# The first layer's activation: ScalarE reads the product bank twice, VectorE adds from SBUF, GpSimd's step is gone

## The chip, the cores and the metric

The kernel runs on one core of a Trainium2 chip. Its time is the device time of one execution, in microseconds (us). The time before is the median of three runs; the profile is of one more execution.

## What is computed

Three stages follow one another. The first is a delta-rule attention over 4 batches, 8 heads, 768 steps and 48 features per head, worked in twelve chunks of 64 steps. Its output, 3072 tokens of 384 features, goes through two feed-forward layers with 2048 hidden features each. The change touches the activation of the first of them:

```python
def _moe_ref(x, w_in, w_out):
    h = x @ w_in                                    # 3072x384 by 384x2048
    g = np.where(h > 0.0, h, 1.0 * (np.exp(np.minimum(h, 0.0)) - 1.0))
    return g @ w_out                                # 2048x384

def _moe2_ref(x, w_in, w_out, a, b):
    h = x @ w_in
    P = a[0] + a[1]*h + a[2]*h*h + a[3]*h*h*h
    Q = 1.0 + abs(b[0])*abs(h) + abs(b[1])*h*h
    return (P / (Q + 1e-6)) @ w_out
```

## The kernel before

The tokens are cut into six windows of 512 (two chunks each). While the first layer works on window w, the attention of window w+1 (`chain`, lines 401 to 556) and the preparation of window w+2 (`g_list` and the recurrence `t_pieces`, lines 267 to 374) run in between. The second layer comes after the sixth window.

In a window the 2048 hidden features are 16 blocks of 128, counted by f. For each block five functions are called:

- `H` (line 581) multiplies: nine matmuls of 512 columns (lines 577 to 579), because operands are split into a high and a low part, into a bank of `h_a`. Its two banks (and in the sixth window a third, `h_c`) are used in turn; both banks of `h_a` are one tile.
- `A1` (line 601): ScalarE reads the bank and writes e = relu(-h) (line 605), then e = exp(-e) (line 606); GpSimd, called POOL, subtracts one in place (line 607).
- `B1` (line 609): VectorE reads the bank again and writes e = max(h, 0) + e (line 612). This is the last read of the bank.
- `C1` (line 614): ScalarE rounds e to gh (line 618), VectorE writes the remainder gl = e - gh (line 620). In the second window POOL writes it for half of the blocks.
- `O` (line 588) multiplies gh and gl with the block of the second weight: nine matmuls (lines 595 to 597) that accumulate in three banks `o`. It stands about two blocks behind `H`.

`e`, `gh` and `gl` have two buffers each. `wo_split` (line 563) splits a block of the second weight for `O` (ScalarE, line 70, and POOL, line 71). Weights arrive as 64-bit numbers; `conv_x`, `conv_d` and `conv_s` (lines 154 to 195) turn them into 32-bit ones with ScalarE, VectorE and, for the first layer, POOL. The second layer's weights are turned in the windows: w_out in windows two to five, w_in all in the sixth.

Each call has a due time in the table `Q` and the loops of lines 811 to 871; the calls are sorted by it. Up to the first steps of the second layer a scheduler then puts the instructions of each engine in order, by due order and its own estimate of when an engine is free, so a change of one instruction can move others. Each engine runs its list strictly in order.

Of the kernel before, what the change touches and what calls it, by code (L numbers as in the profile page):

```python
# [7 lines left out]
F32 = mybir.dt.float32  # L8
# [3 lines left out]
AF = mybir.ActivationFunctionType  # L12
ALU = mybir.AluOpType
# [23 lines left out]
def kernel(  # L37
# [16 lines left out]
    nc = tc.nc  # L54
    mm = nc.tensor.matmul
    act = nc.scalar.activation
# [4 lines left out]
    mp = ctx.enter_context(tc.tile_pool(name="mp", bufs=2))  # L61
# [506 lines left out]
    hp = {}  # L568
# [30 lines left out]
    et = {}  # L599

    def A1(key, f, NC):
        ps = hp[key, f][:, 0:NC]
        e = mp.tile([128, 512], F32, tag="e", name="e")[:, 0:NC]
        et[key, f] = e
        act(out=e, in_=ps, func=AF.Relu, scale=-1.0)  # L605
        act(out=e, in_=e, func=AF.Exp, scale=-1.0)  # L606
        nc.gpsimd.tensor_scalar(out=e, in0=e, scalar1=1.0, scalar2=-1.0, op0=ALU.mult, op1=ALU.add)  # L607

    def B1(key, f, NC):
        ps = hp.pop((key, f))[:, 0:NC]  # L610
        e = et[key, f]
        nc.vector.scalar_tensor_tensor(out=e, in0=ps, scalar=0.0, in1=e, op0=ALU.max, op1=ALU.add)  # L612

    def C1(key, f, NC):
        e = et.pop((key, f))
        gh = mp.tile([128, 512], F32R, tag="gh", name="gh")
        gl = mp.tile([128, 512], F32R, tag="gl", name="gl")
        act(out=gh[:, 0:NC], in_=e, func=AF.Copy)  # L618
        eng = nc.gpsimd if (f % 4 < Q["pg0"] if key == 0 else key == 1 and f % 4 < Q["pg1"]) else nc.vector
        eng.tensor_tensor(out=gl[:, 0:NC], in0=e, in1=gh[:, 0:NC].bitcast(F32), op=ALU.subtract)  # L620
        gt[key, f] = gh, gl
# [189 lines left out]
    for w in range(NW):  # L811
        T = 16 * w
        NC = 256 * len(WINS[w])
        at(T + Q["sx"], split_x, w)
        for f in range(NF):
            at(T + f, lambda w=w, f=f, NC=NC: H(w, f, xt[w], NC))
            at(T + f + .05, A1, w, f, NC)
            at(T + f + Q["b1"], B1, w, f, NC)
            at(T + f + Q["c1o"], C1, w, f, NC)
            at(T + f + Q["ws"], wo_split, w, f)  # L820

            def o1(w=w, f=f, NC=NC):
                t = oring.pop((w, f))
                O(w, f, t[:, 0], t[:, 1], NC)
            at(T + (f + 2.4 if f < NF - 2 else f + 1.95 if f == NF - 2 else f + 1.4), o1)
# [145 lines left out]
```

## Time and profile before

| | us |
|---|---|
| median of three runs | 1167.28 (1157.68 to 1171.71) |
| the profiled execution | 1167.12 |
| its span, first to last instruction | 1165.3 |
| first layer, six windows | about 114 to 758 of the span |
| second layer | about 758 to 1165 |
| TensorE, VectorE, ScalarE, POOL busy | 1061.5, 899.7, 740.7, 520.4 |

PE is TensorE's matmuls, PEld its weight loads, DVE VectorE, ACT ScalarE. A row of waits names the engine and line that stood idle, the one that released it, the total, how often, and the longest. In a row of the timeline the idle time before it stands in brackets. Matmuls overlap: each is shown with 0.39 us while the next one starts 0.23 us after it, so a short stall of TensorE shows in the weight loads rather than in the matmuls.

### The profile page before, as it was taken

Reading aid. Unit: us, or ns where it says so; the run is one execution under the profiler, and the core shown is the slowest. Engines: PE = TensorE matmul, PEld = TensorE weight load, DVE = VectorE, ACT = ScalarE, POOL = GpSimd, SP = SyncE. Lnnn points to the kernel's source line nnn. Section 1 sums busy time; section 2 is a strip of 40 time slices with the busy share of each in tenths; the row PEclk is TensorE's granted clock in tenths of the full one; section 3 lists DMA queues with packets and bytes.
Section 4 is the critical chain, followed back from the end, with each engine's and each line's share of the span. In section 5 each row is a group of like instructions: output and inputs, shape, how many; then the busy total and the mean of one; then the engine's idle time right before and its main releaser. Section 6 shows DMA issues by size and latency. Waiting matters only on the chain.

```text
span 1165.3 us, 20668 instructions
## 1 busy us (share of the span) xinstructions
PE 1061.5 (91%) x7952; PEld 843.8 (72%) x7952; DVE 899.7 (77%) x1231; ACT 740.7 (64%) x1425; POOL 520.4 (45%) x496
## 2 busy tenths in 40 slices
PE   7179887898898999998999998999999999999997
PEld 7055676676687778786777766778787888878785
DVE  4987859768955883696343369999999999999996
ACT  5566666666476546554564578976766667666664
POOL 1484737433444343342443356646363454536332
PEclk8567879998899999998999999999999999999999
DMA  9534424363454122320212044400101001010000
GB/s 278 156 122 152 137 77 131 100 193 100 119 167 149 48 73 89 99 72 8 78 40 67 1 129 136 123 28 1 55 1 30 26 1 55 1 55 1 28 1 27
DMA packets 51842, 91.75 MB, mean 79 GB/s; under 512 B 7072, under 2 KB 29728, under 8 KB 51744
## 3 DMA queue, kind: packets, MB, share of 16 engines
q1 hardware_dynamic: 51744, 90.43, 25.2%
q8 instruction: 62, 1.02, 0.4%
q14 instruction: 36, 0.29, 0.1%
HBM read 77.83 MB, written 12.58 MB: 78 GB/s over the span
## 4 chain that ended last, share of the span: by engine, by line
PE 52%; DVE 23%; issue 7%; ACT 6%; DMA 6%; POOL 5%; POOLq 0%; SPq 0%; DVEq 0%; ACTq 0%
PE o L719 11%; PE h_a L577 6%; PE h_a L578 6%; PE h_a L579 6%; DVE tmp L344 4%; PE o L595 3%; PE o L596 3%; PE o L597 3%; DVE wo L691 2%; PE gp L278 2%; DVE tt L345 2%; PE cb L459 2%; PE h_b L579 2%; PE h_b L577 2%; PE h_b L578 2%
## 5 line engine op out<-in xcount | busy, mean ns | idle before, releaser
L705 POOL TENSOR_TENSOR gl<-wo 128x1024 fp32r<-128x1024 f32 x48 | 146.1, 3043 | 218.4 <-DVE wo L704 187.2
L577 PE MATMUL h_a<-xh,wi 128*128 128x512 f32 x417 | 177.8, 426 | 36.9 <-DVE e L612 33.4
L578 PE MATMUL h_a<-xl,wi 128*128 128x512 f32 x417 | 169.9, 407 | 1.4 <-DVE xl L396 1.4
L579 PE MATMUL h_a<-xh,wi 128*128 128x512 f32 x417 | 169.3, 406 | 0.0
L607 POOL TENSOR_SCALAR e<-e 128x512 f32<-128x512 f32 x96 | 65.8, 685 | 213.2 <-ACT e L606 208.3
L719 PE MATMUL o<-gh,wo 128*128 128x512 f32 x576 | 142.3, 395 | 6.7 <-ACT ys L724 6.4
L71 POOL TENSOR_TENSOR wor<-wo,wor 128x384 fp32r<-128x384 f32 x96 | 103.9, 1083 | 81.2 <-ACT wor L70 74.7
L719 PEld LDWEIGHTS o<-gh,wo 128*128 128x128 f32 x576 | 107.8, 189 | 33.7 <-ACT ys L724 11.1
L612 DVE SCALAR_TENSOR_TENSOR e<-h_a,e 128x512 f32<-128x512 f32 x91 | 62.5, 687 | 89.7 <-POOL e L607 89.0
L577 PEld LDWEIGHTS h_a<-xh,wi 128*128 128x128 f32 x417 | 81.8, 196 | 64.9 <-DVE e L612 41.7
L595 PE MATMUL o<-gh,wor 128*128 128x512 f32 x288 | 119.2, 414 | 0.2 <-ACT gh L618 0.2
L596 PE MATMUL o<-gl,wor 128*128 128x512 f32 x288 | 115.4, 401 | 3.0 <-DVE gl L620 3.0
L597 PE MATMUL o<-gh,wor 128*128 128x512 f32 x288 | 114.2, 397 | 0.0
L605 ACT ACTIVATE e<-h_a 128x512 f32<-128x512 f32 x91 | 54.1, 595 | 89.8 <-PE h_a L579 89.1
L620 DVE TENSOR_TENSOR gl<-e,gh 128x512 fp32r<-128x512 f32 x88 | 74.7, 849 | 29.2 <-ACT gh L618 28.7
L578 PEld LDWEIGHTS h_a<-xl,wi 128*128 128x128 f32 x417 | 82.0, 197 | 17.6 <-DVE xl L396 3.0
L579 PEld LDWEIGHTS h_a<-xh,wi 128*128 128x128 f32 x417 | 81.7, 196 | 18.0
L692 ACT ACTIVATE wo<-wo 128x1024 f32<-128x1024 f32 x48 | 51.0, 1064 | 65.4 <-DVE wo L691 65.4
L691 DVE SCALAR_TENSOR_TENSOR wo<-wo 128x1024 f32<-128x1024 f32 x48 | 75.9, 1582 | 8.5 <-ACT wo L684 8.5
L618 ACT ACTIVATE gh<-e 128x512 fp32r<-128x512 f32 x96 | 60.2, 627 | 32.4 <-DVE e L612 30.7
L70 ACT ACTIVATE wor<-wo 128x384 fp32r<-128x384 f32 x96 | 49.7, 519 | 47.3 <-PE o L597 42.3
L719 PE MATMUL o<-gl,wo 128*128 128x512 f32 x288 | 74.9, 396 | 2.7 <-POOL gl L705 2.7
(162 smaller groups left out, 2474.9 us busy)
## 6 DMA issues: line engine op xcount, KB each, us to landing
kv<-c_kv SPq DMA_DIRECT2D x24, 576.0 KB, 4.3
gin<-g_in SPq DMA_DIRECT2D x69, 192.0 KB, 2.8
kq<-c_kq SPq DMA_DIRECT2D x22, 512.0 KB, 3.8
raw<-w_out SPq DMA_DIRECT2D x42, 192.0 KB, 2.6
raw<-w_in SPq DMA_DIRECT2D x34, 192.0 KB, 2.4
wo<-w_in SPq DMA_DIRECT2D x30, 192.0 KB, 3.0
xr<-x2d SPq DMA_DIRECT2D x6, 768.0 KB, 5.8
out_t<-ys SPq DMA_DIRECT2D x18, 256.0 KB, 2.2
```

The lines of the kernel that those rows point to most:

```text
L71: eng.tensor_tensor(out=t[:, 1], in0=src, in1=t[:, 0].bitcast(F32), op=ALU.subtract)
L577: mm(out=ps, lhsT=hi, rhs=xh[:, c, 0:NC], start=(c == 0), stop=False)
L578: mm(out=ps, lhsT=hi, rhs=xl[:, c, 0:NC], start=False, stop=False)
L579: mm(out=ps, lhsT=lo, rhs=xh[:, c, 0:NC], start=False, stop=(c == 2))
L595: mm(out=ps[:, 0:NC], lhsT=hi[:, cs], rhs=gh[:, 0:NC], start=(f == 0), stop=False)
L596: mm(out=ps[:, 0:NC], lhsT=hi[:, cs], rhs=gl[:, 0:NC], start=False, stop=False)
L597: mm(out=ps[:, 0:NC], lhsT=lo[:, cs], rhs=gh[:, 0:NC], start=False, stop=(f == NF - 1))
L607: nc.gpsimd.tensor_scalar(out=e, in0=e, scalar1=1.0, scalar2=-1.0, op0=ALU.mult, op1=ALU.add)
L620: eng.tensor_tensor(out=gl[:, 0:NC], in0=e, in1=gh[:, 0:NC].bitcast(F32), op=ALU.subtract)
L691: v.scalar_tensor_tensor(out=sq, in0=sq, scalar=1.0 + 1e-6, in1=ab, op0=ALU.add, op1=ALU.add)
L705: nc.gpsimd.tensor_tensor(out=gl, in0=sq, in1=ab, op=ALU.mult)
L719: mm(out=ps, lhsT=wo2[2 * j + i][:, int(p == 1), cs], rhs=(gl if p == 2 else gh)[:, n], start=(j == 0 and p == 0 and i == 0), stop=(j == N ...
```

## The change

`A1` has ScalarE read the bank a second time, for p = relu(h) into a new tile `pe` with two buffers, ahead of the exponential. POOL's subtraction is gone. `B1` reads e and p, both in SBUF, and writes (e - 1) + p; it no longer reads the bank. In the changed kernel the two reads are lines 606 and 607 and the exponential is line 608; lines 612, 618 and 620 keep their numbers.

```diff
     def A1(key, f, NC):
-        ps = hp[key, f][:, 0:NC]
+        ps = hp.pop((key, f))[:, 0:NC]
         e = mp.tile([128, 512], F32, tag="e", name="e")[:, 0:NC]
-        et[key, f] = e
+        p = mp.tile([128, 512], F32, tag="pe", name="pe")[:, 0:NC]
+        et[key, f] = e, p
         act(out=e, in_=ps, func=AF.Relu, scale=-1.0)
+        act(out=p, in_=ps, func=AF.Relu)
         act(out=e, in_=e, func=AF.Exp, scale=-1.0)
-        nc.gpsimd.tensor_scalar(out=e, in0=e, scalar1=1.0, scalar2=-1.0, op0=ALU.mult, op1=ALU.add)
 
     def B1(key, f, NC):
-        ps = hp.pop((key, f))[:, 0:NC]
-        e = et[key, f]
-        nc.vector.scalar_tensor_tensor(out=e, in0=ps, scalar=0.0, in1=e, op0=ALU.max, op1=ALU.add)
+        e, p = et[key, f]
+        nc.vector.scalar_tensor_tensor(out=e, in0=e, scalar=-1.0, in1=p, op0=ALU.add, op1=ALU.add)
 
     def C1(key, f, NC):
-        e = et.pop((key, f))
+        e, _ = et.pop((key, f))
```

The lists of the engines change in two ways that matter here. On TensorE, in the second window before block 12, the block's first matmul (`wi_1880` is the block's weight, `gp` a product of the preparation, `o` the accumulators) waits before for VectorE:

```order
L596 MATMUL o_2893<-gl,wor 128x512
L597 MATMUL o_2893<-gh,wor 128x512
L278 MATMUL gp<-gin 128x128 [waits DMAHW0_49,PE_49]
L278 MATMUL gp<-gin 128x128
L278 MATMUL gp<-gin 128x128 [waits DMAHW1_49]
L278 MATMUL gp<-gin 128x128
L577 MATMUL h_a<-xh,wi_1880 128x512 [waits DVE_49]
```

and now, with the block's weight under the name `wi_1888`, for ScalarE:

```order
L596 MATMUL o_2912<-gl,wor 128x512
L597 MATMUL o_2912<-gh,wor 128x512
L278 MATMUL gp<-gin 128x128 [waits DMAHW0_49,PE_49]
L278 MATMUL gp<-gin 128x128
L278 MATMUL gp<-gin 128x128 [waits DMAHW1_49]
L278 MATMUL gp<-gin 128x128
L577 MATMUL h_a<-xh,wi_1888 128x512 [waits Activation_49]
```

The neighbours are the same; from the second to the fifth window `H`, `O` and the pieces of `chain` keep nearly the same order on TensorE, while in the first and the sixth some trade places. The wait in front of `H` has passed from VectorE to ScalarE.

On ScalarE, in the sixth window, one block before reads (`raw` are weights being turned, `wor` and `wo` splits of second weights, `wi` splits of the second layer's first weight):

```order
L605 ACTIVATE e<-h_a 128x512
L161 ACTIVATE raw_7574<-raw_7574 128x192
L606 ACTIVATE e<-e 128x512
L70 ACTIVATE wor<-wo_94 128x384
L70 ACTIVATE wi_7680<-ce 128x192
L159 ACTIVATE raw<-raw 128x192
L161 ACTIVATE raw<-raw 128x192
L70 ACTIVATE wi_7680<-ce 128x192
L618 ACTIVATE gh<-e 128x512
L605 ACTIVATE e<-h_c 128x512
```

and now a block reads:

```order
L606 ACTIVATE e<-h_a 128x512
L607 ACTIVATE pe<-h_a 128x512
L608 ACTIVATE e<-e 128x512
L159 ACTIVATE raw<-raw 128x192
L161 ACTIVATE raw<-raw 128x192
L70 ACTIVATE wi_7710<-ce 128x192
L70 ACTIVATE wo_7740<-w2r 128x384
L159 ACTIVATE raw_7661<-raw_7661 128x192
L161 ACTIVATE raw_7661<-raw_7661 128x192
L70 ACTIVATE wor<-wo_94 128x384
L70 ACTIVATE wi_7769<-ce 128x192
L618 ACTIVATE gh<-e 128x512
```

The two reads stand side by side with the exponential right behind them, and nearly every block of that window now has this same list of twelve.

## Rows read from the trace of the kernel before

**Rows 1.** Busy time by stretch: three of the six windows, the second layer; last three rates

```profile
core 0: us, PE busy (x) PEld busy (x) DVE busy (x) ACT busy (x) POOL busy (x), PEclk, DMA share, GB/s
114.00:256.00 142.00, 121.51 (x1111) 94.97 (x1110) 105.68 (x195) 93.34 (x258) 72.88 (x94) 0.88 0.44 134
...
583.00:674.00 91.00, 90.52 (x947) 71.79 (x946) 32.65 (x48) 51.41 (x96) 31.56 (x39) 1.00 0.11 35
674.00:758.00 84.00, 77.17 (x327) 60.10 (x326) 71.77 (x113) 73.00 (x183) 52.41 (x64) 1.00 0.44 134
758.00:1165.00 407.00, 393.16 (x1703) 319.70 (x1701) 378.70 (x291) 269.83 (x274) 179.79 (x80) 0.99 0.07 22
```

**Rows 2.** Waits of all engines, first layer (114 to 758 us)

```profile
DVE e L612 <- POOL e L607: 89.0, 47, 4.0
...
PEld h_a L577 <- DVE e L612: 41.7, 34, 5.0
...
PEld o L596 <- DVE gl L620: 5.6, 7, 1.4
```

**Rows 3.** The wait of `H`, in the first, second, fourth and sixth window

```profile
PEld h_a L577 <- DVE e L612: 13.9, 9, 5.0
...
PEld h_a L577 <- DVE e L612: 8.5, 8, 4.9
...
PEld h_a L577 <- DVE e L612: 4.9, 3, 3.6
...
PEld h_a L577 <- DVE e L612: 9.0, 8, 1.7
```

**Rows 4.** Timeline of 576 to 579 us: one block's activation and the next `H`

```profile
576.15 0.60 ACT L605 ACTIVATE e<-h_a 128x512 f32<-128x512 f32 x1 [0.93 <-PE h_a L579]
...
576.78 0.63 ACT L606 ACTIVATE e<-e 128x512 f32<-128x512 f32 x1
...
577.50 0.62 POOL L607 TENSOR_SCALAR e<-e 128x512 f32<-128x512 f32 x1 [0.47 <-ACT e L606]
...
578.15 0.69 DVE L612 SCALAR_TENSOR_TENSOR e<-h_a,e 128x512 f32<-128x512 f32 x1 [1.81 <-POOL e L607]
...
578.89 0.19 PEld L577 LDWEIGHTS h_a<-xh,wi 128*128 128x128 f32 x1 [0.49 <-DVE e L612]
```

**Rows 5.** Timeline of ScalarE, VectorE and TensorE, 188 to 197 us: a long wait

```profile
188.98 0.58 ACT L605 ACTIVATE e<-h_a 128x512 f32<-128x512 f32 x1
...
193.24 1.62 DVE L344 TENSOR_TENSOR tmp<-tt,am 128x1024 f32<-128x1024 f32 x1
194.88 0.69 DVE L612 SCALAR_TENSOR_TENSOR e<-h_a,e 128x512 f32<-128x512 f32 x1
...
195.63 0.79 PE L577 MATMUL h_a<-xh,wi 128*128 128x512 f32 x1 [4.60 <-DVE e L612]
```

**Rows 6.** Busy time by stretch behind three long waits; columns as in rows 1

```profile
196.00:200.00 4.00, 4.00 (x12) 3.12 (x12) 3.90 (x7) 1.92 (x6) 0.00 (x0) 0.63 0.16 57
...
312.00:316.00 4.00, 2.17 (x5) 1.78 (x6) 3.97 (x5) 1.29 (x3) 1.05 (x1) 0.50 0.26 74
...
534.00:538.00 4.00, 4.00 (x41) 2.98 (x42) 3.35 (x4) 1.39 (x3) 0.62 (x1) 0.64 0.00 0
```

**Rows 7.** The costliest groups of instructions, whole span: busy us, mean ns

```profile
L612 DVE SCALAR_TENSOR_TENSOR e<-h_a,e 128x512 f32<-128x512 f32 x91 | 62.5, 687 | 89.7 <-POOL e L607 89.0
L605 ACT ACTIVATE e<-h_a 128x512 f32<-128x512 f32 x91 | 54.1, 595 | 89.8 <-PE h_a L579 89.1
L620 DVE TENSOR_TENSOR gl<-e,gh 128x512 fp32r<-128x512 f32 x88 | 74.7, 849 | 29.2 <-ACT gh L618 28.7
```

**Rows 8.** Lines 612 and 620 on VectorE: shortest, median and longest in ns

```profile
L612 DVE SCALAR_TENSOR_TENSOR e<-h_a,e x91: 671/692/694, 125.4 to 746.0; 128x512 f32<-128x512 f32 x91
...
L620 DVE TENSOR_TENSOR gl<-e,gh x88: 641/694/1576, 129.3 to 757.1; 128x512 fp32r<-128x512 f32 x88
```

**Rows 9.** Timeline near 563 us: line 620 beside work of POOL

```profile
562.43 1.01 POOL L71 TENSOR_TENSOR wor<-wo,wor 128x384 fp32r<-128x384 f32 x1 [2.39 <-ACT wor L70]
...
562.90 1.09 DVE L620 TENSOR_TENSOR gl<-e,gh 128x512 fp32r<-128x512 f32 x1 [2.14 <-ACT gh L618]
```

## The prediction

> **What bounds the kernel now.** I read the busy times by stretch first, to find where the change can matter, then the waits of the first layer, then two timelines of single blocks.
>
> The stretches [rows 1] show that the second layer takes 407 us with VectorE busy for 378.70 of them; none of its lines is edited, so I carry it over. The first layer takes the 644 us from 114 to 758. Its first window is the slowest: 142 us, in which TensorE is busy for 121.51 and VectorE for 105.68. In the fifth window TensorE is busy for 90.52 of 91 us and nothing else comes near it. In the sixth, 84 us, ScalarE (73.00) and VectorE (71.77) are as full as TensorE (77.17), because the second layer's weights are turned there.
>
> The waits [rows 2] name the largest loss on TensorE: the weight load of `H` stands 41.7 us, in 34 pieces, behind VectorE's line 612, the last reader of the bank. By window it is 13.9 us in the first, 8.5 in the second, 4.9 in the fourth, 9.0 in the sixth [rows 3]. The later use of the same block, `O` waiting for gl, costs only 5.6 us [rows 2].
>
> One block shows why [rows 4]. ScalarE begins to read at 576.15; the exponential, POOL's step and VectorE's addition follow, and line 612 ends at 578.15 + 0.69 = 578.84. The next `H` loads its weight at 578.89. So the next block waits for the block just before it, although its own bank is the other one of the two; the tile is treated as one. From the start of the reading to the release pass 2.69 us, and `O`, nine matmuls at 0.23, covers only about 2.1 of them; a piece of `chain`, where one stands there, covers the rest.
>
> A long wait looks different [rows 5]. ScalarE reads at 188.98, but line 612 runs at 194.88, behind the recurrence's steps in VectorE's list (one of 1.62 us directly ahead), and TensorE loses 4.60 us. Behind such waits TensorE's granted clock is 0.63, 0.50 and 0.64 in slices of 4 us [rows 6], between its two levels of 1.2 and 2.4 GHz, against 1.00 in the fifth window [rows 1].
>
> **The change part by part.** The sum is made against the profiled execution's 1167.1 us, which is also the median of the runs.
>
> *Release of the bank.* The bank is free after two reads of 0.595 us each [rows 7], about 1.2 us from the first read's start instead of 2.69, and no longer behind POOL's and VectorE's lists. In the long wait above it would be free by about 190.2, before TensorE had run dry. At most the 41.7 - 9.0 = 32.7 us of the first five windows go [rows 2, 3]. What is late next is gl: `O` of a block stands behind two further `H`, so TensorE may run some 5 us ahead of VectorE, and the few waits for gl today say that this room is hardly used. But VectorE's own work stays, and in the recurrence stretches it is nearly full (3.90 and 3.97 of 4 us) [rows 6]. A part of each long wait therefore comes back as a wait for gl, or for a free e buffer. Bounds: nothing to 32.7 us. I take three quarters, 24.5, since many pieces are short and lie where VectorE has time.
>
> *Clock.* Of the slices above, 0.63 and 0.50 of full speed cost 4 x 0.37 = 1.5 and 4 x 0.50 = 2.0 us if TensorE is the limit there. Five long waits of 1 to 2 us make 5 to 10; as part of that time is idle anyway I take 4, between 0 and 10.
>
> *ScalarE's second read.* 96 reads of 0.595 us are 57 us. In the first five windows ScalarE is at 66% (93.34 of 142) or lower, down to 56% (51.41 of 91) [rows 1], so 80 x 0.595 = 47.6 us lie in its gaps; what queues behind a read is the copies of `chain`, and TensorE's list has matmuls of `H` and `O` ahead of their use. I charge 2 us, with 0 and 47.6 as ends; if the gaps were not there, all of it would be paid. In the sixth window 16 x 0.595 = 9.5 us meet 84 - 73.00 = 11.0 us of idle time, part of which is waits that stay. ScalarE becomes the limit: with 4 us of idle left, 73.0 + 9.5 + 4 = 86.5, so 2.5 us are paid (0 to 9.5), and the 9.0 us of `H` waits there bring nothing.
>
> The second read also adds a wait: `pe` has two buffers, so block n+2's read needs line 612 of block n, and the exponential and the copies of `chain` stand behind it in ScalarE's list. The first read, just ahead, already needs line 620 of block n for its e buffer, which runs later than line 612; so the new wait is never the last, and I count nothing for it.
>
> *VectorE's addition.* It swaps a bank operand for one in SBUF. With a bank operand it takes 671 to 694 ns, never more; line 620, with two SBUF operands of the same size, takes 641 to 1576 [rows 8], and its mean is 849 against 687 [rows 7]. The difference shows beside POOL: at 562.90 line 620 takes 1.09 us while POOL works from 562.43 to 563.44 [rows 9]. So line 612 may cost 0.16 us more, 96 x 0.162 = 15.6 us of VectorE. Against it, POOL loses 96 steps of about 0.62 us [rows 4], each of which could hold VectorE's other two-operand instructions; that excess could shrink by as much. It counts where VectorE is full, in the recurrence stretches and the sixth window. I charge 3 us, between -15 and +15.6.
>
> The Trainium skill, "SBUF — State Buffer", section "SBUF: two separate sides", says that VectorE and GpSimd share a pair of ports as an exclusive lock: an operation with two SBUF inputs and a GpSimd one that reads SBUF exclude each other for the whole instruction. The trace agrees (1.09 us beside POOL's work, against a median of 0.694). By that rule the new form of line 612 can be blocked by up to one POOL instruction, which the old could not; the rival below is this mechanism.
>
> The Trainium skill, "ScalarE: Activation LUTs", section "Rules for kernel authors", puts relu on VectorE. By that rule the second read is on the wrong engine; in these rows one read of a bank costs 0.595 us on ScalarE and 0.687 on VectorE, so it names no loss here but ScalarE's fullness.
>
> *POOL's step and the moved lists.* Removing POOL's 0.62 us and its hand-over shortens the way to gh by about what the second read adds; I count nothing, covered by the room ahead of `O`. Loads move in the lists too; the DMA engines are at most 44% busy in a window [rows 1], so I count nothing, and 3 us if a load comes late.
>
> Sum: -24.5 - 4 + 2 + 2.5 + 3 = -21; rounded with the profiled 1167.1: 1146.
>
> **The rivals.**
>
> *All of it comes, clock included.* For it: `O` hardly waits for gl today. Against it: VectorE is full where the long waits are. 1167.1 - 32.7 - 10 + 2.5 = 1127.
>
> *The wait moves to gl and the e buffers.* VectorE's lists are the limit in the first four windows, and TensorE gains only the short pieces, perhaps 12 us; 1167.1 - 12 + 2.5 + 2 = 1160. For it: VectorE's 3.9 of 4 us in those slices; against it: its 105.68 of 142 over the whole first window.
>
> *The port between VectorE and POOL.* Line 612 is held as long as line 620 is, in the stretches that VectorE limits and in the rest: the full 15.6 in place of 3 gives 1146 + 12.6 = 1159. For it: 0.849 against 0.687; against it: POOL is emptier by 60 us.
>
> *Slower: ScalarE becomes the queue.* Each read stands in ScalarE's list ahead of copies that release TensorE, so that all 57 us are paid, while the 41.7 us are won and VectorE's 15.6 are lost: 1167.1 + 57 - 41.7 + 15.6 = 1198. It decides from the point where ScalarE has under 0.6 us free per block. For it: 73.00 of 84 in the sixth window; against it: 66% and less elsewhere.
>
> **How the numbers follow.** Forecast 0.45 (1135 to 1156), everything 0.20, wait moved 0.18, port 0.10, slower 0.07. About 2%, 23 us, is what a measurement of this kernel can tell from no change; the line is 1144. Faster by more: 0.20 and 0.23 of the forecast's half, 0.43. Slower by more, above 1190: 0.04 of the last rival. Between: 0.53. The range leaves out the best cases beyond 1122 and the last rival: 1122 to 1172.
>
> **What would show it.** Right: weight loads of `H` wait under 10 us, and for ScalarE; line 607 runs 0.60 us right behind line 606; line 612 on VectorE has a mean between 0.70 and 0.85 and a longest well over 0.694; the first window is 8 to 12 us shorter, the fifth by 1 to 2, the sixth is 86 to 88 us with ScalarE over 80 of them; waits of `O` for gl rise from 5.6 to some 10 us. Wrong: `H` waits as long for ScalarE as it did for VectorE, or waits for gl exceed 25 us, or the second layer changes by over 3 us.

## The result and the profile after

The changed kernel takes 1148.68 us (median; 1144.03 to 1153.02), beside 1165.87 for the kernel before in the same runs. The ratio is 0.986, with a 95% interval of 0.982 to 0.991: about 16 us less, under the 2% that the forecast took as its line. The profiled execution takes 1144.03 us with a span of 1142.2 (before 1167.12 and 1165.3) and is the fastest of its four, so the traces differ by 23 us where the medians differ by 17.

The busy times by stretch of the kernel after (columns as in [rows 1]; the six windows and the second layer):

```profile
114.00:244.00 130.00, 116.00 (x1117) 91.71 (x1118) 107.60 (x191) 98.19 (x270) 65.62 (x79) 0.92 0.46 141
244.00:362.00 118.00, 104.83 (x1075) 84.33 (x1074) 90.45 (x172) 79.91 (x199) 41.56 (x38) 0.96 0.47 143
...
567.00:655.00 88.00, 87.75 (x942) 71.08 (x941) 34.46 (x48) 56.06 (x111) 22.71 (x22) 1.00 0.11 36
655.00:737.00 82.00, 78.57 (x335) 62.52 (x334) 70.80 (x114) 78.75 (x198) 40.08 (x47) 0.98 0.45 138
737.00:1142.00 405.00, 390.11 (x1695) 317.74 (x1693) 375.01 (x289) 268.74 (x273) 179.85 (x80) 0.99 0.06 22
```

Against [rows 1] the first window is 130 us for 142, the fifth 88 for 91, the sixth 82 for 84, the second layer 405 for 407. The borders of these stretches are off by up to 4 us. Measured from the first weight load of `H` in a window to that in the next (in the sixth to the last load of `O`), the six windows take 143.6, 119.5, 107.9, 99.6, 88.7 and 85.6 us before and 130.1, 116.7, 106.0, 99.0, 88.1 and 83.9 after. So 13.5 of the 21.1 us of the first layer are won in the first window. The second won 2.8, which its stretches do not show; this is the row of the kernel before for it:

```profile
256.00:374.00 118.00, 108.23 (x1078) 86.22 (x1078) 86.24 (x166) 73.96 (x180) 49.82 (x55) 0.93 0.46 136
```

The waits of the first layer, kernel after (who stood idle, for whom, us in total, times, longest):

```profile
DVE e L612 <- ACT e L608: 75.7, 42, 5.1
ACT gh L618 <- DVE e L612: 33.7, 20, 4.2
PEld h_a L577 <- ACT pe L607: 13.7, 9, 3.0
PEld cb L459 <- DVE R L451: 13.1, 13, 2.8
PEld h_a L578 <- DVE xl L396: 7.8, 9, 1.7
PEld o L596 <- DVE gl L620: 3.3, 6, 1.6
```

`H` waits 13.7 us for ScalarE where it waited 41.7 for VectorE; from the start of the first read to the end of the second pass 1.09 us on average. `O` waits 3.3 us for gl where it waited 5.6 [rows 2]. Two rows have grown: the load of `cb` in `chain` waits 13.1 us for VectorE's R (line 451), and the second load of `H` waits 7.8 us for xl, VectorE's low part of the window's tokens (line 396). The same waits of the kernel before, with that of ScalarE's gh:

```profile
ACT gh L618 <- DVE e L612: 30.7, 29, 4.5
...
PEld cb L459 <- DVE R L451: 3.3, 2, 2.3
...
PEld h_a L578 <- DVE xl L396: 3.0, 3, 1.7
```

The edited lines on the page of the kernel after (columns as in [rows 7]), and VectorE's addition among its shortest, median and longest (as [rows 8]):

```profile
L612 DVE SCALAR_TENSOR_TENSOR e<-e,pe 128x512 f32<-128x512 f32 x96 | 69.3, 722 | 76.0 <-ACT e L608 75.7
...
L620 DVE TENSOR_TENSOR gl<-e,gh 128x512 fp32r<-128x512 f32 x88 | 77.4, 880 | 29.0 <-ACT gh L618 28.6
```

```profile
L612 DVE SCALAR_TENSOR_TENSOR e<-e,pe x96: 637/692/1523, 125.0 to 726.3; 128x512 f32<-128x512 f32 x96
```

### The profile page after: what moved, and what is told of

It reads as the page before. It is cut to its first block, busy times and chain, and to the rows that moved or that the text cites. A ratio compares the mean times of both kernels' runs of the same rounds, so it can differ in the third digit from the quotient of the medians.

```text
span 1142.2 us, 20625 instructions
## 1 busy us (share of the span) xinstructions
PE 1046.1 (92%) x7952; PEld 836.8 (73%) x7952; DVE 903.3 (79%) x1231; ACT 772.3 (68%) x1521; POOL 464.1 (41%) x400
## 4 chain that ended last, share of the span: by engine, by line
PE 53%; DVE 26%; ACT 7%; issue 7%; DMA 4%; POOL 4%; SPq 0%; POOLq 0%; DVEq 0%; ACTq 0%
PE o L719 12%; PE h_a L577 6%; PE h_a L578 5%; PE h_a L579 5%; DVE tmp L344 5%; PE o L595 3%; PE o L596 3%; PE o L597 3%; PE gp L278 2%; DVE tt L345 2%; PE h_b L577 2%; PE h_b L578 2%; PE h_b L579 2%; DVE wo L691 2%; DVE e L612 1%
## 5 line engine op out<-in xcount | busy, mean ns | idle before, releaser
L71 POOL TENSOR_TENSOR wor<-wo,wor 128x384 fp32r<-128x384 f32 x96 | 108.8, 1135 | 264.8 <-ACT wor L70 257.2
L577 PE MATMUL h_a<-xh,wi 128*128 128x512 f32 x417 | 174.2, 418 | 11.1 <-ACT pe L607 11.0
L579 PE MATMUL h_a<-xh,wi 128*128 128x512 f32 x417 | 168.2, 403 | 0.0
L719 PEld LDWEIGHTS o<-gh,wo 128*128 128x128 f32 x576 | 107.8, 189 | 33.0 <-ACT ys L724 10.8
L612 DVE SCALAR_TENSOR_TENSOR e<-e,pe 128x512 f32<-128x512 f32 x96 | 69.3, 722 | 76.0 <-ACT e L608 75.7
L595 PE MATMUL o<-gh,wor 128*128 128x512 f32 x288 | 116.4, 412 | 0.0
L597 PE MATMUL o<-gh,wor 128*128 128x512 f32 x288 | 113.2, 393 | 0.0
L577 PEld LDWEIGHTS h_a<-xh,wi 128*128 128x128 f32 x417 | 80.8, 194 | 31.6 <-ACT pe L607 13.7
L620 DVE TENSOR_TENSOR gl<-e,gh 128x512 fp32r<-128x512 f32 x88 | 77.4, 880 | 29.0 <-ACT gh L618 28.6
L618 ACT ACTIVATE gh<-e 128x512 fp32r<-128x512 f32 x96 | 60.1, 626 | 33.7 <-DVE e L612 33.7
L702 DVE SCALAR_TENSOR_TENSOR gh<-wo,ab_sb 128x1024 fp32r<-128x1024 f32 x48 | 65.3, 1359 | 8.1 <-ACT wo L693 2.0
```

The costliest lines, as they stand in the source:

```text
L71: eng.tensor_tensor(out=t[:, 1], in0=src, in1=t[:, 0].bitcast(F32), op=ALU.subtract)
L577: mm(out=ps, lhsT=hi, rhs=xh[:, c, 0:NC], start=(c == 0), stop=False)
L579: mm(out=ps, lhsT=lo, rhs=xh[:, c, 0:NC], start=False, stop=(c == 2))
L595: mm(out=ps[:, 0:NC], lhsT=hi[:, cs], rhs=gh[:, 0:NC], start=(f == 0), stop=False)
L597: mm(out=ps[:, 0:NC], lhsT=lo[:, cs], rhs=gh[:, 0:NC], start=False, stop=(f == NF - 1))
L612: nc.vector.scalar_tensor_tensor(out=e, in0=e, scalar=-1.0, in1=p, op0=ALU.add, op1=ALU.add)
```

## The experiments

The change does three things at once: the bank comes free early, ScalarE reads once more, and POOL's step leaves the way from the bank to gl. The runs take them apart. Another way to free the bank early is a tile for each of its two banks, so that a block no longer waits for the one just before it. Ratios are to the kernel before in the same runs, with 95% intervals; differences in us are the ratio's (1165.87 times its distance from 1), here and in the text, since the median of before moved by some 3 us from group to group. "Read to gh" is the mean time from the start of the first read of a bank to the start of the rounding gh, over the 80 blocks of the first five windows. "Windows 1 to 5" and "window 6" are us from the first weight load of `H` to that in the sixth window, and from there to the last load of `O`. These three columns are worked out from the timeline of the one traced execution. It lies within 5 us of the kernel's median but for e5, whose traced execution (1153.82) is the fastest of its twelve; that of the kernel before (1167.12) is 1 to 4 us above its medians.

| kernel | tiles | reads by ScalarE | POOL's step | median us | ratio | us | read to gh, us | windows 1 to 5 | window 6 |
|---|---|---|---|---|---|---|---|---|---|
| before | one | one | on e | 1165.87 | 1 | 0 | 4.02 | 559.3 | 85.6 |
| after | one | two | gone | 1148.68 | 0.986 (0.982 to 0.991) | -16 | 3.98 | 539.9 | 83.9 |
| e1 | one | two | on e | 1175.56 | 1.014 (1.008 to 1.020) | +16 | 4.89 | 553.3 | 96.5 |
| e2 | one | one | gone | 1158.01 | 0.997 (0.993 to 1.002) | -3 | 3.69 | 548.8 | 82.2 |
| e3 | two | one | on e | 1155.55 | 0.995 (0.991 to 0.999) | -6 | 4.46 | 540.6 | 84.6 |
| e4 | two | two | gone | 1150.57 | 0.989 (0.986 to 0.993) | -12 | 3.97 | 540.9 | 83.4 |
| e5 | one | two | on p | 1164.12 | 1.000 (0.997 to 1.003) | 0 | 4.26 | 550.7 | 89.1 |
| e6 | two | one | gone | 1147.13 | 0.987 (0.984 to 0.990) | -15 | 3.92 | 535.7 | 86.4 |
| e7 | one | three | gone | 1161.58 | 0.997 (0.994 to 1.000) | -4 | 4.42 | 547.9 | 91.4 |
| e8 | one | two in the first window | gone there | 1157.35 | 0.995 (0.992 to 0.997) | -6 | 4.02 | 546.0 | 85.9 |
| e9 | two | one | in the split | 1147.69 | 0.988 (0.984 to 0.992) | -14 | 4.00 | 538.4 | 86.4 |
| e10 | two | two | on e | 1179.27 | 1.015 (1.009 to 1.021) | +17 | 4.93 | 566.0 | 95.2 |
| e11 | one | two | on 8 columns | 1159.02 | 0.996 (0.992 to 0.999) | -5 | 4.22 | 549.7 | 87.5 |
| e12 | two | two | on e, O later | 1183.07 | 1.017 (1.012 to 1.022) | +20 | 5.39 | 564.1 | 94.7 |

### e1 to e4: the parts alone

e1, the two reads with POOL's step kept (against the kernel before; `B1` adds 0 in place of minus one):

```diff
         act(out=e, in_=ps, func=AF.Relu, scale=-1.0)
+        act(out=p, in_=ps, func=AF.Relu)
         act(out=e, in_=e, func=AF.Exp, scale=-1.0)
         nc.gpsimd.tensor_scalar(out=e, in0=e, scalar1=1.0, scalar2=-1.0, op0=ALU.mult, op1=ALU.add)
...
+        nc.vector.scalar_tensor_tensor(out=e, in0=e, scalar=0.0, in1=p, op0=ALU.add, op1=ALU.add)
```

> The changed kernel with POOL's step kept (POOL subtracts one, VectorE adds the two SBUF operands): only the early release of the bank is left of the change. Theory (the gain is the bank that ScalarE frees): weight loads of H wait 10 to 20 us for ScalarE as in the changed kernel (13.7), the time is 1145 to 1156. Rival (the gain is POOL's hand-over that is gone from the way to gh, and POOL's time): 1160 to 1170, as the kernel before.

1175.56 us: slower than the kernel before, which neither theory had. `H`'s loads wait 20.4 us, near what the theory said.

e2, POOL's step taken out of the kernel before (so the minus one is left out of the result, in e6 as well):

```diff
-        nc.gpsimd.tensor_scalar(out=e, in0=e, scalar1=1.0, scalar2=-1.0, op0=ALU.mult, op1=ALU.add)
```

> The kernel before without POOL's step (the subtraction of one is left out altogether); VectorE still frees the bank. Theory: the release comes about 0.7 us earlier per block, but stays in VectorE's list; weight loads of H wait 25 to 38 us (41.7 before), 1153 to 1165. Rival (POOL's hand-over is the gain): 1140 to 1152, and H waits under 20 us.

1158.01 us; the ratio's interval includes 1. `H` still waits 42.9 us for VectorE, more than the 25 to 38 of the theory, whose time came true. Taking POOL off the way does not by itself free the bank.

e3 and e4, a tile for each bank in the first five windows, in the kernel before and in the changed one:

```diff
-        ps = h_c if i == 2 else h_a[:, i]
+        ps = h_1[i] if h_c is None else h_c if i == 2 else h_a[:, i]
```

> The kernel before with the two banks of h_a as two tiles in the first five windows, so that H waits only for the block before the last. Theory (the two banks are treated as one, and that alone makes H wait for the block just before): the waits of H for line 612 fall from 41.7 us to under 12 (nearly all in the sixth window), and the time to 1135 to 1152. Rival (VectorE's list is the limit, the wait only moves to gl): waits of H fall, those of O for gl rise by over 15 us, 1158 to 1168.

1155.55 us, between the two theories. The waits of `H` fall to 16.8 us (8.7 for the new tiles, 8.1 for `h_a` in the sixth window), as by the change, and yet only 6 us are won; `cb` waits 16.8 us for R where it waited 3.3 before. The trace holds a second reason. Its first layer is nearly as short as the changed kernel's (625.2 against 623.8 us), but from the last load of `O` to the end of the span, where no instruction is edited, it takes 411.2 us, against 403.2 to 408.4 in the other traces. TensorE waits there for ScalarE's copies of the output (10.8 us in the changed kernel), which wait for the output before to be stored:

```profile
PEld o L719 <- ACT ys L724: 13.8, 11, 3.9
```

How much of the distance from e3 to the changed kernel and to e6 lies in the activation, one trace cannot tell.

> The changed kernel with two tiles as well. Theory: the last 13.7 us of H waiting for ScalarE go, and of them about half is won: 1137 to 1147. Rival (what is left is the recurrence and chain through VectorE): 1146 to 1152, with u1's waits for line 451 above 15 us.

1150.57 us. In the waits of the first layer `H`'s first load has 0.2 us left for a bank, and the time is the changed kernel's. So the 13.7 us of `H` waits that the changed kernel has left are not what holds it; `cb` waits 12.7 us for R (the rival, whose time came true, had said over 15) and `O` 7.5 us for gl.

What makes e1 slow is sought first in its waits (first layer; the addition is line 613 there, gh line 619, gl line 621):

```profile
ACT gh L619 <- DVE e L613: 73.9, 48, 7.8
PEld h_a L577 <- ACT pe L607: 20.4, 12, 4.2
PEld o L596 <- DVE gl L621: 16.1, 15, 2.0
...
PEld o L595 <- ACT gh L619: 8.2, 11, 1.9
```

`H` waits less than before, but ScalarE stands 73.9 us before gh, where the kernel before had 30.7 and the changed one 33.7, and `O` waits 24.3 us for gl and gh. One block of e1's timeline shows the way (start, duration, engine, line; idle time and releaser in the bracket); first ScalarE, then POOL, then VectorE:

```profile
413.99 0.63 ACT L608 ACTIVATE e<-e 128x512 f32<-128x512 f32 x1
...
423.37 0.63 ACT L619 ACTIVATE gh<-e 128x512 fp32r<-128x512 f32 x1 [7.79 <-DVE e L613]
423.91 0.58 ACT L606 ACTIVATE e<-h_a 128x512 f32<-128x512 f32 x1
```

```profile
415.52 0.83 POOL L421 TENSOR_TENSOR kv<-kv,n_t 128x384 f32<-128x384 f32 x1 [4.39 <-DMA kv<-c_kv]
416.32 0.62 POOL L609 TENSOR_SCALAR e<-e 128x512 f32<-128x512 f32 x1
```

```profile
417.40 2.40 DVE L344 TENSOR_TENSOR tmp<-xx_t,tt 128x768 f32<-128x768 f32 x1
419.83 0.95 DVE L345 TENSOR_REDUCE tt<-tmp 128x64 f32<-128x768 f32 x1
420.82 1.92 DVE L344 TENSOR_TENSOR tmp<-xx_t,tt 128x1024 f32<-128x1024 f32 x1
422.65 0.69 DVE L613 SCALAR_TENSOR_TENSOR e<-e,pe 128x512 f32<-128x512 f32 x1
```

The exponential ends at 414.62. POOL's step begins at 416.32, behind a `kv` that had waited for its load, and ends at 416.94. The addition starts at 422.65, behind steps of the recurrence (the last three are shown), and ScalarE, whose next entry is gh, idles 7.79 us with the next block's reads behind gh. The same place of the kernel after:

```profile
406.20 1.62 DVE L344 TENSOR_TENSOR tmp<-xx_t,tt 128x768 f32<-128x768 f32 x1
407.86 0.95 DVE L345 TENSOR_REDUCE tt<-tmp 128x64 f32<-128x768 f32 x1
408.49 1.01 POOL L71 TENSOR_TENSOR wor<-wo,wor 128x384 fp32r<-128x384 f32 x1
408.73 1.32 DVE L612 SCALAR_TENSOR_TENSOR e<-e,pe 128x512 f32<-128x512 f32 x1
409.97 2.10 DVE L344 TENSOR_TENSOR tmp<-xx_t,tt 128x1024 f32<-128x1024 f32 x1
410.08 0.64 ACT L618 ACTIVATE gh<-e 128x512 fp32r<-128x512 f32 x1 [2.91 <-DVE e L612]
```

Here the addition stands ahead of the 1024-wide step, and ScalarE idles 2.91 us. With POOL's step kept, the addition stands behind one more step in VectorE's list, and most of the wait in e1 is that place (5.71 us from the end of POOL's step) and not POOL's 0.62 us.

That is not all of e1's loss. Of the 26.0 us by which its first layer is longer than the changed kernel's, 12.6 lie in the sixth window (the table's last column), where neither the recurrence nor `chain` runs. This is the window and its waits:

```profile
669.10:765.60 96.50, 85.23 (x340) 64.61 (x339) 78.67 (x117) 81.18 (x198) 55.05 (x63) 0.97 0.39 117
```

```profile
PEld o L596 <- DVE gl L621: 11.4, 9, 2.0
...
ACT wi L70 <- DVE ce L176: 9.8, 12, 0.9
DVE raw L175 <- ACT raw L161: 8.2, 11, 1.2
...
ACT gh L619 <- DVE e L613: 3.1, 4, 1.5
```

gh waits 3.1 us here. What grew is the turning of the second layer's weights, in which ScalarE and VectorE wait for each other, and VectorE's own work (78.67 us for 72.70: its subtraction in the split of the second layer's weights, 15 times, takes 1.015 us on average for 0.570). e10 and e12 lose 11 to 12 us in this window against e4. No run took this part by itself.

### e5 to e8: length, price and place

e5 keeps POOL's minus one, but on p, beside the exponential:

```diff
         act(out=e, in_=e, func=AF.Exp, scale=-1.0)
+        nc.gpsimd.tensor_scalar(out=p, in0=p, scalar1=1.0, scalar2=-1.0, op0=ALU.mult, op1=ALU.add)
```

> The changed kernel, with POOL's minus one kept, but on p = relu(h) instead of on e: it runs beside the exponential and no longer between it and VectorE's addition. In the run with the two reads and POOL's step kept on e (1175.56 us), ScalarE's rounding gh stood idle 73.9 us for VectorE's e, and the reads of the next block stood behind it in ScalarE's list (at 425.02 us of that run the block's first load waits 4.02 us, after ScalarE had waited 7.79 us for e). Theory (the two reads bring the bank early only if the way from e to gh is short, since gh stands ahead of the next reads in ScalarE's list): POOL's step is off the way, gh waits 35 to 50 us, H's loads under 20 us, time 1146 to 1158 us. Rival (POOL's 55 us of work, or the lists that it moves, are what the earlier run paid for, wherever the step stands): gh waits over 60 us and the time stays at 1165 to 1178 us.

1164.12 us, between the two: 16 us better than e1, 16 worse than the changed kernel. VectorE still waits for POOL, gh waits 51.2 us, and `H`'s loads wait 15.2, which the theory had right and which again did not decide the time. These waits are those of its fastest execution.

e6 joins e2 and e3: a tile for each bank, no POOL step, VectorE reads the bank last.

> The kernel before with a tile for each bank and without POOL's minus one (which is left out; the addition stays as it is, VectorE still reads the bank last). The two parts alone gave 1155.55 us (ratio 0.995) and 1158.01 us (0.9973). Theory (the bank's release and the short way from e to gh need each other; who reads last is not the point): together more than their sum, 1143 to 1151 us, H's loads waiting under 15 us. Rival 1 (the parts only add up): 1151 to 1156 us. Rival 2 (the release must come from ScalarE, since VectorE's list with the recurrence in it is what is late): H's loads still wait over 25 us, 1156 to 1162 us.

1147.13 us, the same as the changed kernel, with ScalarE reading once. The theory's range held it: the parts gave 6 and 3 us alone and 15 together. Who reads last does not decide the time. The waits of the first layer of e6 (addition line 611, gh line 617, gl line 619):

```profile
ACT gh L617 <- DVE e L611: 26.6, 17, 4.3
PEld cb L459 <- DVE R L451: 11.9, 8, 2.1
PEld h_a L577 <- DVE e L611: 8.3, 6, 3.3
PEld o L596 <- DVE gl L619: 2.6, 3, 1.3
```

e7 adds a third read to the changed kernel:

```diff
         act(out=p, in_=ps, func=AF.Relu)
+        act(out=p, in_=ps, func=AF.Relu)
```

> The changed kernel with p = relu(h) written twice from the bank, so that the bank comes free 0.48 us later and ScalarE has 96 times some 0.48 to 0.60 us, 46 to 57 us, more to do. It prices what the second read costs. Theory (ScalarE's time is nearly free in the first five windows, and sets the end only in the sixth, where it is busy 78.75 of 82 us): the sixth window grows by 5 to 9 us, the others by 0 to 6 together, time 1154 to 1164 us. Rival (a read on the way to the release costs in every window): each of the first five grows by 3 us or more, time 1168 us or more. Second rival (ScalarE has room everywhere): under 1153 us.

1161.58 us: 13 us for 47.0 us of ScalarE's busy time (819.3 against 772.3). It does not price a read alone. The third read stands behind the exponential in ScalarE's list (in 95 of 96 blocks), so the bank comes free some 1.0 us later and not 0.48 (2.09 us from the first read's start to the last one's end, 1.09 in the changed kernel), and VectorE's addition now waits for that read (102.5 us in the first layer). The time is in the theory's range, but the place only in part: the sixth window grew from 83.9 to 91.4 us, as said, while the first five together grew by 8.0 where the theory had at most 6 (the first by 11.0, and the third and fourth gave 5.0 back). Waits of `O` for gl and gh rise to 13.5 us.

e8 makes the change in the first window alone:

```diff
+        if key == 0:
+            p = mp.tile([128, 512], F32, tag="pe", name="pe")[:, 0:NC]
+            act(out=p, in_=ps, func=AF.Relu)
```

> The change in the first window alone; the other five keep the activation of before (one read, POOL's step, VectorE frees the bank). Of the 22 us between the two profiled executions, the first window gave 12. Theory (the gain is local to the window in which the bank was awaited): the first window 128 to 132 us, the rest as before, time 1151 to 1159 us. Rival (the first window's 12 us are its start and the order that the scheduler happens to find; part is given back where the pieces that were late wait again in the second window): time 1160 us or more.

1157.35 us, in the theory's range; the ratio, 0.995, is worth 6 us of the changed kernel's 16. In its trace the first window takes 133.5 us (143.6 before, 130.1 in the changed kernel; the theory said 128 to 132), and the last load of `O` starts 12.2 us earlier than before (747.6 against 759.8 us): the first window's gain stays.

### e9 to e12: the whole computation the other way, and why the slow ones are slow

e9 is e6 with the minus one put into the split:

```diff
-        act(out=gh[:, 0:NC], in_=e, func=AF.Copy)
+        act(out=gh[:, 0:NC], in_=e, func=AF.Copy, bias=-1.0)
...
+            nc.vector.scalar_tensor_tensor(out=gl[:, 0:NC], in0=e, scalar=-1.0, in1=gh[:, 0:NC].bitcast(F32), op0=ALU.add, op1=ALU.subtract)
```

> The whole computation again, by the way that the last runs point to: a tile for each bank, VectorE adds max(h, 0) + exp from the bank as before, POOL's step is gone, and the minus one goes into the split: gh = e - 1 by ScalarE's copy with a bias, gl = (e - 1) - gh in one VectorE instruction (on POOL, for 8 blocks of the second window, two). ScalarE reads the bank once. Against the run without POOL's step at all (1147.13 us) the only cost is what a bias and a second operation add to instructions that exist anyway. Theory (nothing there: the split's instructions cost the same): 1144 to 1151 us, the same as the changed kernel or a little better. Rival (the two-operand form with a scalar, whose longest ones took 1.5 us where the plain subtraction's rows of before show the same, is slower on VectorE, or the eight blocks on POOL hold O up): gl's mean over 0.95 us, 1151 us or more.

1147.69 us, as the theory had it, and no better than the changed kernel (intervals 0.984 to 0.992 and 0.982 to 0.991). gl's mean is 917 ns against 880. It does with 96 reads and a tile fewer what the change does.

e10 is e1 with a tile for each bank, and so e4 with POOL's step kept.

> The run of two reads with POOL's step kept (1175.56 us), with a tile for each bank besides. It is the last of the eight combinations of tiles, reads and POOL's step. Theory (what makes the two reads with POOL's step slow is ScalarE's list: gh waits for VectorE's late addition and the next reads stand behind it; with a tile for each bank the matmuls need a bank only a block later, so the reads may be late): H's loads wait under 8 us, gh still over 55 us, time 1156 to 1166 us. Rival (the slowness is in the way to O, through gl and gh, and has nothing to do with the bank): H's loads under 8 us and yet 1168 to 1178 us.

1179.27 us: the rival, a little above its range. The waits of the first layer of e10:

```profile
ACT gh L619 <- DVE e L613: 69.4, 44, 7.3
PEld cb L459 <- DVE R L451: 21.6, 13, 5.6
PEld o L596 <- DVE gl L621: 21.1, 22, 2.0
...
PEld o L595 <- ACT gh L619: 8.2, 12, 1.5
...
PEld h_a L577 <- ACT pe L607: 0.3, 1, 0.3
```

`H` waits 0.3 us for a read of the bank, and the run is 30 us slower than e4. My theory of e1, that the late reads cost by way of the bank, falls: the waits sit in `O` (29.3 us, 15.2 of them in the sixth window) and in `chain` (21.6 us).

e11 is e1 with POOL's step on 8 of 512 columns:

```diff
-        nc.gpsimd.tensor_scalar(out=e, in0=e, scalar1=1.0, scalar2=-1.0, op0=ALU.mult, op1=ALU.add)
+        nc.gpsimd.tensor_scalar(out=e[:, 0:8], in0=e[:, 0:8], scalar1=1.0, scalar2=-1.0, op0=ALU.mult, op1=ALU.add)
```

> The run of two reads with POOL's step kept (1175.56 us), but POOL's step takes 8 of the 512 columns (the other 504 keep e without the minus one): the hand-over to POOL and the place in its list stay, its time goes. From the end of the exponential to the start of VectorE's addition lay 1.83 us on average with the whole step (94 blocks seen), 0.67 us in the changed kernel without one. Theory (most of it is POOL's 0.6 us, and the recurrence steps that VectorE's list then takes ahead of the addition): exponential to addition 0.6 to 1.1 us, gh waits under 50 us, time 1148 to 1160 us. Rival (the hand-over through a third list is the cost, whatever the step's length): exponential to addition over 1.3 us, gh waits over 60 us, time 1164 us or more.

1159.02 us, at the far end of the theory's range; from the exponential's end to the addition pass 1.09 us on average in the first five windows (e1 1.98, the changed kernel 0.77). Of the 32 us between e1 and the changed kernel, 21 go with POOL's time on the data, and 11 stay with the hand-over to a third list and the 0.20 us (median) that the short step takes.

e12 moves `O` later in e10's TensorE list:

```diff
-            at(T + (f + 2.4 if f < NF - 2 else f + 1.95 if f == NF - 2 else f + 1.4), o1)
+            at(T + (f + 2.85 if f < NF - 2 else f + 1.95 if f == NF - 2 else f + 1.4), o1)
```

> The slowest run (a tile for each bank, two reads, POOL's step kept; 1179.27 us) with O's due time moved from 2.4 to 2.85 blocks behind H, which puts the pieces of chain that stood behind O on TensorE's list ahead of it. In that run H's loads no longer waited for a read of the bank, while O's waited 25.3 us for gl and gh (18.4 and 6.9 us; 3.3 us for gl in the changed kernel). Theory (the slow runs are slow because the way from the bank to gl is too long for O's place in the list): O's loads wait under 14 us for gl and gh, time 1158 to 1171 us. Rival (the way is what costs wherever O stands, since two buffers of gh and gl, or the engines' lists behind it, hold everything to the same pace): time 1173 us or more, and O's waits turn up in front of chain or H instead.

1183.07 us, the rival's time. Waits of the first layer of e12:

```profile
PEld o L596 <- DVE gl L621: 23.7, 21, 2.0
...
PEld o L595 <- ACT gh L619: 7.9, 12, 1.2
```

`O` waits 31.6 us although it stands later, and not `chain` or `H` in its stead, as the rival had it: gl and gh fell back with it, and read to gh grew to 5.39 us.

What is left as the account, argued and not shown: in the lists of ScalarE the gh of a block stands ahead of the reads of the next (in 76 to 79 of the 79 pairs of the first five windows in every trace). Where gh has to wait, the next reads wait behind it, whatever tiles the banks have and wherever `O` stands. In the table the kernels with an early bank (all but before, e2 and e8) fall into three groups by "read to gh": 3.92 to 4.00 us give 1147 to 1151, 4.22 to 4.46 give 1156 to 1164, 4.89 to 5.39 give 1176 to 1183. Their first five windows take 535.7 to 540.9, 547.9 to 550.7 and 553.3 to 566.0 us, with one exception: e3, whose 4.46 us go with 540.6. In the first five windows of the kernel before, the gh right ahead of a read idled 11 times, but each of these reads then waited another 1.8 us or more for its own product, so gh held none of them. In the changed kernel 7 such gh, idle for 17.8 us, were followed at once by the read that they had held, in e1 10, idle for 32.2. A product (counted as done 0.58 us after its last weight load starts, 0.19 for the load and 0.39 for the matmul) lies 0.3 us on average until it is read in the kernel before, 0.9 in the changed one, 1.1 in e1. Two things stand outside this account: e3, and the 11 to 13 us that e1, e10 and e12 lose in the sixth window. That the order gh before reads is the cause was not tried on its own: no run put gh behind the next block's reads.

## Why the prediction held, and which steps did not

The forecast of 1146 missed the median by 3 us, with the first window 12 us shorter (8 to 12 was said), line 607 right behind 606, line 612 at a mean of 0.722 us (0.70 to 0.85) with a longest of 1.523, and the second layer within 2 us. Inside the sum two terms were off, and they cancelled, so that the number came out is in part luck. By the runs, taken in this order, the 16 us are: early bank 6 (e3), POOL's step 9 more (e3 to e6), the second read 3 back (e6 to e4); the 4 that are left (e4 to after) lie within the intervals. In another order the parts have other prices, as the terms below show.

*Release of the bank, -24.5.* The release itself came as said (1.09 us from the first read's start, about 1.2 said); what it is worth was put too high. The bank's waits did go, from 41.7 to 13.7 us (under 10 was said), but 9.8 us came back at `cb` and 4.8 at the second load of `H` (rows above), a net 13.4. An early bank alone is worth 6 us (e3), and with POOL's step gone 12 (e2 to e6). The step "comes back as a wait for gl, or for a free e buffer" failed: waits for gl fell to 3.3 us where some 10 were said. What came back waits for VectorE's other results, R and xl.

*POOL's step, 0.* Too small, and for the reason that the prediction gave itself: the step's removal "shortens the way to gh by about what the second read adds". That was right in size (read to gh 4.02 before, 3.98 after) and priced wrongly, because each half is large. With POOL's step kept, the second read makes the kernel 16 us slower than before (e1), and 23 slower than one read does (e3 to e10). POOL's step costs 3 us next to one read with a late bank (before to e2, not told from nothing), 9 next to one read with an early bank (e3 to e6; of the 7.8 us between the spans of these two traces 3.1 lie in the first layer), 30 to 32 next to two reads (e4 to e10, after to e1). "Covered by the room ahead of `O`" was no cover: with the step kept, `O` waits 24.3 us for gl and gh (e1) and 29.3 (e10).

*ScalarE's second read, +2 and +2.5.* Between e6 and e4 it costs 3 us, with overlapping intervals; in their traces it costs 5.2 in the first five windows and gives 3.0 back in the sixth, where both banks of `h_a` are still one tile. The third read costs 13, later release included. The rows of the first five windows were read too high: ScalarE's share goes down to 52% in the fourth (51.93 of 100 us), not to 56%. In the sixth window a size was off and not the mechanism: the window is 82 us and not 86 to 88, with ScalarE busy for 78.75, which is 96% of it. Its busy time grew by 5.8 us, not 9.5, in part since two reads in a row start 0.48 to 0.50 us apart; and the third read, which adds to ScalarE, made the window 7.5 us longer. The 9.0 us of `H` waits there, which were to "bring nothing", went. The Trainium skill, "ScalarE: Activation LUTs", section "Rules for kernel authors", puts relu on VectorE: e6 and e9, which keep it there, are as fast as the changed kernel, so the rule is neither borne out nor gainsaid by these times.

*Clock, -4.* Not shown. The granted clock rose in the first window from 0.88 to 0.92 and in the second from 0.93 to 0.96, but it does not order the runs: over the whole span e6 has 0.939 and e9 0.938, as the kernel before (0.937), and they are as fast as the changed kernel with 0.947.

*VectorE's addition, +3.* It measured 0.722 against 0.687 us: 96 x 0.035 = 3.4 us, not the 15.6 of the port rival. The Trainium skill, "SBUF — State Buffer", section "SBUF: two separate sides", lets an addition with two SBUF operands be shut out by POOL. The trace bears it out: 7 of the 96 are longer than 0.75 us. In each of them an instruction of POOL had started before and ran on for 0.22 to 0.97 us, and the addition ended 0.54 to 0.55 us after it, as at 408.73 above, where POOL ends at 409.50 and the addition at 410.05. Of the 89 others 24 lie beside POOL as well; in 18 of these VectorE had started first, and in 6 POOL had started at the same time (within 0.01 us) or ended within 0.20 us. So the hold is no matter of chance, but few additions met it.

*The second window.* It gained 2.8 us, though 8.5 us of `H` waits stood there [rows 3]; the forecast named nothing for it. The fifth, which was to gain 1 to 2, gained 0.6 (88.7 to 88.1). The second window's timeline, ScalarE of the kernel after, shows reads held by a gh that waits for VectorE and by a copy that waits for a load, with `H` waiting 2.97 us behind them at 291.46:

```profile
286.39 0.63 ACT L618 ACTIVATE gh<-e 128x512 fp32r<-128x512 f32 x1 [2.81 <-DVE e L612]
287.43 0.39 ACT L159 ACTIVATE raw<-raw 128x192 f32<-128x192 f32 x1 [0.41 <-DMA raw<-w_out]
...
289.81 0.38 ACT L159 ACTIVATE raw<-raw 128x192 f32<-128x192 f32 x1 [1.74 <-DMA raw<-w_out]
...
290.36 0.57 ACT L606 ACTIVATE e<-h_a 128x512 f32<-128x512 f32 x1
290.83 0.58 ACT L607 ACTIVATE pe<-h_a 128x512 f32<-128x512 f32 x1
```

The slower rival, ScalarE as the queue (0.07), did not come. e1 and e10, the same second read with POOL's step left in, are slower than the kernel before, by 16 and 17 us, but there ScalarE idles before gh (73.9 and 69.4 us) more than it lacks time.

## What to carry to other kernels

A wait names the resource that came last, not what it is worth: kernels here that took away 21 to 41 us of the same wait ended between 16 us faster and 20 us slower, and the longer one block's way through the lists of the engines was, the slower they were, with one exception. When a step is added to such a way, it is worth counting the whole way against the step that stands in front of the next block in each list, and taking as much out as goes in; here that is the reading of the runs which fits best, not one that was tried alone. Where two accumulators are used in turn, try a tile for each before giving an engine a second read: here that, with the minus one folded into instructions that exist anyway, gave the same time with 96 instructions fewer on ScalarE.

## What the runs showed of the hardware

Reads of 128x512 that follow each other on ScalarE are shown with 0.595 us on average and start 0.48 to 0.50 us apart (median 0.494), so a group's mean overstates by a fifth the time that one more takes of the engine. VectorE's addition from two SBUF operands has the same median as with a bank operand (0.692 against 0.692 us). POOL's empty time did not help VectorE's other two-operand line: line 620 has a mean of 0.880 us after and 0.849 before, with 39 of 88 over 0.75 us in both, all of them beside work of POOL, although POOL worked 56 us less. An addition that met an instruction of POOL already under way, which still ran for 0.22 us or more, ended 0.54 to 0.55 us after it (7 of 7).
